# Attention and a cosine-gated MLP on one core: first output stage in visits of 2, 2, 2, 1, lower transfer figures in the planner, the last MLP pair in halves, and the inverse sums stored by SyncE

## The chip, the core and the metric

The kernel runs on one core of one Trainium2 chip. The metric is the device time of one execution in microseconds (us). Five engines work side by side and meet only at semaphores: TensorE (PE, matmuls), ScalarE (ACT, activations), VectorE (DVE), GpSimd (POOL) and SyncE (SP, which here only issues transfers). ACT and POOL can issue transfers too. Each engine runs its own list of instructions in order, so an instruction that waits holds everything behind it on that engine.

## What is computed

```python
q_n = q / (norm(q) + 1e-6); k_n = k / (norm(k) + 1e-6)      # (8, 12, 448, 64) each
attn = softmax(q_n @ k_n.T / tau)                           # tau = 0.1
x = (attn @ v) as (8 * 448, 12 * 64) = (3584, 768)
h = x @ w_in                                                # (768, 2048)
out = (h * cos(h)) @ w_out                                  # (2048, 768), float32
```

## The kernel before, in words

**Tiling.** A *quad* is two pairs of heads of one batch; there are 24 quads (NQ), three for each of the eight batches. A quad's 448 keys are seven *groups* of 64 (NJ = 7), numbered g = 7 * quad + j. For each group, `scores` (L551) makes four 64x64-tile matmuls into two PSUM banks and ACT takes the exponential of both banks into one of 17 tiles E (L567); `attend` (L570) multiplies E with V and accumulates the quad's seven groups in banks X and Y (4 and 5). When the quad is complete, DVE copies the result to AVs (L586). Scores go alternately to banks 0, 1 and 2, 3, so PE can be at most two groups ahead of ACT's exponentials.

**Sums.** The softmax's sums are made later, in *rounds* of one or two quads (ROUNDS, L733: quad 3 alone, then 4 and 5, 6 and 7, and so on): `sums` (L630) adds up the E tiles with matmuls against a selector (L642), ACT takes Ln and Exp(-x) of the 448 columns (L649, L651), which gives the inverse sums in Zs, a small transfer stores them in DRAM (rscr, L652), and broadcasting loads bring them back to all partitions as R (L658, two per quad, issued by SP). POOL (DVE for quad 5) then multiplies AVs with R, which gives the quad's part of xT (L662). Quads 0 to 2 go another way in the prologue (`spread`, `scale_x`), using the tiles ar.

**Norms.** For each quad SP loads Q and K (Qf, Kf, L398, 448 KB each), POOL squares (L450), DVE reduces (L454), ACT and DVE make the inverse norms (L480 to L493), POOL scales (L501), and SP turns the result with DMA transposes into qT and kT (`turn`, L539, L544). A quad's turn may begin when the scores of the quad two before it are done, since there are two qT and kT.

**MLP.** For each batch c, `m1_part` (L670) makes 16 blocks of h (128 hidden columns each, six matmuls a block, L676) in eight pairs of banks, and `m1` (L683) makes h * cos(h) of a pair of blocks with four instructions over both banks: ACT rounds h / 2 pi to an integer (L689), DVE subtracts (L691), ACT takes the sine (L693), DVE multiplies into gT (L695). `m2` (L698) multiplies gT with w_out, 16 matmuls for each output tile of 128 rows and half of the columns (L704); DVE copies the tile out (L722) and SP stores it (L728).

**Order.** PE's order is the program's. After the prologue (quads 0 to 2), stage c does the MLP's first product of batch c, then its *output stage*: *visits*, each made by `group` (L756), of up to two groups of scores with the attends of the visit before, and between the visits `fill` (L953) puts matmuls of `m2`, and the sums that are due. QUADS (L731) gives the quads begun in each stage: 5, 4, 3, 3, 3, 3, 0, 0. In the first stage (c = 0) the visits cover groups 21 to 55: one group, then 17 times two, so quads of seven groups are straddled by every second visit (L975). There 20 matmuls of `m2` come first, 8 after the first visit, and 4 after each of the others. After the first visit of that stage the squares of a spare quad are added and `norm_b` of quad 5 is put in the list (L981). A round becomes due when a visit starts a quad (L773).

The other engines' order is made by a list scheduler, `Planner` (L22): every operation has an estimated duration, a latency and a priority worked back from PE's order; a transfer's estimate is 1.2 us, its `moves` figure and 0.8 us (FIRST, LAST), its ring being one of SP, ACT and POOL (`land`, L70). SWITCH (L32) is the estimated cost of a change between matmul shapes on PE. The estimates do not reach the chip: they only set the order in which ACT, DVE, POOL and SP get their instructions, and where semaphores are waited for. `lead` (15 for the sums' operations) raises a priority.

Of the kernel before, what the change touches and what calls it, by code (L numbers as in the profile page):

```python
# [8 lines left out]
ACT = mybir.ActivationFunctionType  # L9
# [12 lines left out]
class Planner:  # L22
# [6 lines left out]
    ENGINES = ("pe", "act", "dve", "pool", "sp")  # L29
    HOP = {"pe": 0.055, "act": 0.045, "dve": 0.035, "pool": 0.08, "sp": 0.15}  # L30
    LAT = {"pe": 0.165, "act": 0.103, "dve": 0.085, "pool": 0.045, "sp": 0.0}
    SWITCH = 0.093  # L32
    FIRST, LAST = 1.2, 0.8
    WORTH = 1.0

# [236 lines left out]
def bass_cosine_attention__then__act_gcu_kernel(  # L272
# [110 lines left out]
    def cut(kind, u, part):  # L383

        return [(kind, u, i) for i, (j0, j1) in enumerate(CELLS) if part[0] < j1 and j0 < part[1]]
# [7 lines left out]
    def load_one(qd, w, part=ALL[0], after=(), eng="sp"):  # L393
        b, h0, s = qd // QB, 2 * (qd % QB), qd % 3
        src, dst, nm = ((q, Qf, "Qf"), (k, Kf, "Kf"))[w]
        j0, j1 = part
        ap = bass.AP(src.tensor, (b * NH + h0) * S * D + j0 * D, [[NJ * D, 128], [NH // 2 * S * D, 2], [1, (j1 - j0) * D]])
        return op(eng, 0.5, lambda e: e.dma_start(dst[s].ap()[:, :, j0:j1].rearrange("p r j d -> p r (j d)"), ap),  # L398
                  w=cut(nm, s, part), dma=(nm, s, j0), moves=0.196 * (j1 - j0), after=after, keep=qd > 4)

    def load_qk(qd, after=()):
        return [load_one(qd, w, after=after) for w in range(2)]
# [4 lines left out]
    def load_v(qd, after=()):  # L407
        b, h0, s = qd // QB, 2 * (qd % QB), qd % NV
        ap = bass.AP(v.tensor, (b * NH + h0) * S * D, [[NJ * D, 128], [NH // 2 * S * D, 2], [1, NJ * D]])
        return pool_dma(0.75, lambda e: e.dma_start(Vb[s].ap().rearrange("p r j d -> p r (j d)"), ap),  # L410
                  w=[("V", s)], dma=("V", s), moves=1.67, after=after)

    NW, WARM = 2, 34

    def load_w1(i, hf, after=()):
        w = FF // NW
        if 1:
            src = bass.AP(moe_w_in.tensor, hf * NKC * D * FF + i * w, [[FF, D], [D * FF, NKC], [1, w]])
            dst = W1.ap()[64 * hf:64 * hf + 64, :, i * w:i * w + w]
            return pool_dma(0.69, lambda e, src=src, dst=dst: e.dma_start(dst, src),  # L420
                     w=[("W1", i, hf)], dma=("W1", i, hf), moves=4.26, after=after)

    def load_w2(i, hf):
        src = moe_w_out.rearrange("(f p) n -> p f n", p=128)[:, 8 * i:8 * i + 8, HW * hf:HW * hf + HW]
        return pool_dma(0.79, lambda e: e.dma_start(W2.ap()[:, 8 * i:8 * i + 8, HW * hf:HW * hf + HW], src),
                 w=[("W2", i, hf)], dma=("W2", i, hf), moves=5.18)

    H, NLEAD, FAST = 2 * NJ, 5.0, 7
    SPARE = FIRST + 3
# [109 lines left out]
    def turn(qd):  # L539

        u = qd % 2
        turned[qd] = []
        for n, t, nm in ((Qn, qT, "Q"), (Kn, kT, "K")):
            turned[qd].append(op("sp", 1.3, lambda e, n=n, t=t: e.dma_start_transpose(  # L544
                t[u].ap().rearrange("p j a x -> p j (a x)"), n[u].ap().rearrange("p j r d -> p (j r d)")),
               r=cut(nm + "n", u, ALL[0]), w=cut(nm + "T", u, ALL[0]), dma=(nm + "T", u), moves=1.61, keep=True))

    summed = set()
    holds = {}
# [37 lines left out]

    Z, LEAD = 6, 15.0

    def spread(qd, j0, j1):  # L590

        s = qd % 3
        gs = range(NJ * qd + j0, NJ * qd + j1)

        def mm(e):
            for g in gs:
                for a in range(2):
                    for r in range(2):
                        ins = e.matmul(bank(Z + a, S, 64 * r, 64 * r + 64), ones.ap()[64 * a:64 * a + 64, :],
                                       E[g % NE].ap()[64 * a:64 * a + 64, r, :],  # L600
                                       start=(g == NJ * qd), stop=(g == NJ * qd + NJ - 1))
            return ins

        op("pe", 0.19 * (j1 - j0), mm, r=[("E", g % NE) for g in gs] + ["ones"], w=pair(Z), mode="q")
        if j1 < NJ:
            return
        summed.add(qd)
        act("exp", 0.815, lambda e: e.activation(ar[s].ap(), two(Z), ACT.Ln, bias=0.0, scale=1.0), r=pair(Z), w=[("ar", s)])
        act("exp", 0.83, lambda e: e.activation(ar[s].ap(), ar[s].ap(), ACT.Exp, bias=0.0, scale=-1.0),
            r=[("ar", s)], w=[("ar", s)])  # L610

    def scale_x(qd):
        b, c0, s = qd // QB, 2 * (qd % QB), qd % 3
        op("dve", 1.01, lambda e: e.tensor_tensor(xT[b % 2].ap()[:, c0:c0 + 2, :], two(X), ar[s].ap(), ALU.mult),
           r=pair(X) + [("ar", s)], w=[("x", b % 2, qd % QB)])

    def stir(qd, n):

# [11 lines left out]
    def sums(quads, bk):  # L630
        n = rounds[0]
        rounds[0] += 1
        summed.update(quads)
        z = n % 2
        np_ = 2 * len(quads)
        rows = 2 * np_

        def mm(e):
            for j in range(NJ):
                for i in range(np_):  # L640
                    es = (quads[i // 2] * NJ + j) % NE
                    ins = e.matmul(bank(bk, S, 32 * i, 32 * i + 32), sel.ap(), E[es].ap()[:, i % 2, :],  # L642
                                   start=(j == 0), stop=(j == NJ - 1))
            return ins

        op("pe", 1.32, mm, r=[("E", (qd * NJ + j) % NE) for qd in quads for j in range(NJ)] + ["sel"], w=whole(bk),
           mode="s")
        zz = Zs[z].ap()[0:32 * np_, :]
        act("exp", 0.44, lambda e: e.activation(zz, bank(bk, S, 0, 32 * np_), ACT.Ln, bias=0.0, scale=1.0),  # L649
            r=whole(bk), w=[("Zs", z)], lead=LEAD)  # L650
        act("exp", 0.47, lambda e: e.activation(zz, zz, ACT.Exp, bias=0.0, scale=-1.0), r=[("Zs", z)], w=[("Zs", z)], lead=LEAD)  # L651
        op("act", 0.6, lambda e: e.dma_start(rscr.ap()[8 * n:8 * n + rows, :], Zs[z].ap()[0:32 * np_:16, :]),  # L652
           r=[("Zs", z)], w=[("rs", n)], dma=("rs", z), moves=0.05, lead=LEAD)
        for i, qd in enumerate(quads):
            u, sl, b = qd % 2, qd % NA, qd // QB
            for r in range(2):
                ap = bass.AP(rscr, (8 * n + 4 * i + 2 * r) * S, [[0, 64], [S, 2], [1, S]])
                op("sp", 0.5, lambda e, r=r, u=u, ap=ap: e.dma_start(R[u].ap()[64 * r:64 * r + 64], ap),  # L658
                   r=[("rs", n)], w=[("R", u, r)], after=spared, dma=("R", u, r), moves=0.85, lead=LEAD)
            c0 = 2 * (qd % QB)  # L660
            late = qd == 2 * QB - 1
            op("dve" if late else "pool", 1.02 if late else 2.04, lambda e, u=u, sl=sl, b=b, c0=c0: e.tensor_tensor(  # L662
                xT[b % 2].ap()[:, c0:c0 + 2, :], AVs[sl].ap(), R[u].ap(), ALU.mult),
                r=[("AV", sl), ("R", u, 0), ("R", u, 1)], w=[("x", b % 2, qd % QB)], lead=LEAD)
# [18 lines left out]
    def m1(c, pr, bk):  # L683
        s = pairs[0] % 3
        pairs[0] += 1
        col = S * (c % 2)
        bs = pair(bk)

        op("act", 0.815, lambda e: e.activation(ar[s].ap().bitcast(I32), two(bk), ACT.Identity, bias=0.25, scale=INV2PI),  # L689
           r=bs, w=[("ar", s)])  # L690
        op("dve", 1.005, lambda e: e.scalar_tensor_tensor(ar[s].ap(), ar[s].ap().bitcast(I32), -2.0 * math.pi, two(bk),  # L691
                                                          ALU.mult, ALU.add), r=bs + [("ar", s)], w=[("ar", s)])
        act("sin", 0.86, lambda e: e.activation(ar[s].ap(), ar[s].ap(), ACT.Sin, bias=GUARD * math.pi / 2.0, scale=GUARD),  # L693
            r=[("ar", s)], w=[("ar", s)])
        op("dve", 1.01, lambda e: e.tensor_tensor(gT.ap()[:, 2 * pr:2 * pr + 2, col:col + S], two(bk), ar[s].ap(), ALU.mult),  # L695
           r=bs + [("ar", s)], w=[("g", c % 2, 2 * pr), ("g", c % 2, 2 * pr + 1)])

    def m2(t, h, f0, f1, bk):  # L698
        col = 128 * t % GC
# [10 lines left out]
        if f1 == NNB and t == B * S // 128 - 1:  # L710
# [3 lines left out]
            for sg, eng in enumerate(("sp", "act" if h else "sp")):  # L714
# [1 line left out]
                dst = bass.AP(out.tensor, (S * b + cc // 64) * KM + HW * h, [[NJ * KM, 64], [1, HW]])  # L716
                op(eng, 0.5, lambda e, sg=sg, dst=dst: e.dma_start(
                    dst, osb[so].ap()[64 * sg:64 * sg + 64, HW * h:HW * h + HW]),
                   r=[("o", so, h)], w=[("out", t, sg, h)], dma=("store", t, h, sg), moves=0.32)
        elif f1 == NNB:  # L720
            so = t % 3
            op("dve", 0.475, lambda e: e.tensor_copy(osb[so].ap()[:, HW * h:HW * h + HW], bank(bk, HW)),  # L722
# [1 line left out]
            if h:  # L724
                for sg in range(2):
                    b, cc = divmod(128 * t + 64 * sg, S)
                    dst = bass.AP(out.tensor, (S * b + cc // 64) * KM, [[NJ * KM, 64], [1, KM]])
                    op("sp", 0.5, lambda e, sg=sg, dst=dst: e.dma_start(dst, osb[so].ap()[64 * sg:64 * sg + 64, :]),  # L728
                       r=[("o", so, 0), ("o", so, 1)], w=[("out", t, sg)], dma=("store", so, sg), moves=0.66)

    QUADS = [5, 4, 3, 3, 3, 3, 0, 0]  # L731
    W, MOST = (1, 1), 9
# [186 lines left out]
    for c in range(B):  # L919
# [52 lines left out]
                m2(t, h, f0, f1, bank_of[t, h])  # L972

        new = done + QUADS[c]
        todo = [range(max(g, NJ * done), min(g + 2, NJ * new)) for g in range(NJ * done - (c == 0), NJ * new, 2)]  # L975
        more = new > done
        done = new
        if todo:
# [49 lines left out]
```

## Time and profile before

| | |
|---|---|
| three runs | 442.67, 439.15 and 441.56 us; median 441.56 |
| the profiled execution | 439.9 us, its span 438.3 us |
| granted TensorE clock, mean | 0.996 |
| PE, ACT, DVE, POOL busy | 419.0, 310.9, 255.7, 211.7 us of the span |
| prologue and c = 0's first product | 0 to 56.2 us |
| first output stage (c = 0) | 56.2 to 100.4 us |
| c = 1's first product begins | 101.31 us |
| c = 7's last output matmuls | to 434.5 us |

The table is of one profiled execution; its times are microseconds from the span's start. In the lines of the profile that follow, a line of a timeline has the start, the duration, the engine, the line of the code, the operation, the tile written and the tile read, and in brackets the idle time before it with what ended it. A `q` behind the name of an engine (SPq, ACTq) marks the issue of a transfer, which is not counted as busy time.

### The profile page before, as it was taken

The numbers are of one execution on the slowest core, as the hardware profiler recorded it, in microseconds if no ns is written. First come the engines' busy times: TensorE is split into PE (matmuls) and PEld (weight loads), VectorE is DVE, ScalarE is ACT, GpSimd is POOL, SyncE is SP. The second block draws the span as 40 slices with busy tenths as digits, with TensorE's granted clock in tenths as the row PEclk, the third lists the DMA queues.
The fourth block names the chain that finished last, engine by engine and source line by source line (L and its number), as shares of the span: only waits on it lengthen the run. The fifth ranks groups of instructions, "written<-read, shape, count | busy, mean of one in ns | idle before, by whom it ended". The sixth has DMA issues, their size and how long they took to land.

```text
span 438.3 us, 8435 instructions
## 1 busy us (share of the span) xinstructions
PE 419.0 (96%) x3578; PEld 208.3 (48%) x3578; DVE 255.7 (58%) x300; ACT 310.9 (71%) x432; POOL 211.7 (48%) x145
## 2 busy tenths in 40 slices
PE   7889998989999899999999999999999999999996
PEld 7344542334544345444454454444554445565563
DVE  4865993246972349923696329933585225935931
ACT  4898877897788777788679766878678757704700
POOL 3888545659347778277636773149633033000000
PEclk9999998999999999999999999999999999999999
DMA  7999995797918979276952995067931614021022
GB/s 255 238 255 222 272 193 112 172 224 168 203 55 187 235 167 247 45 167 152 237 159 61 236 237 139 0 137 188 221 71 38 159 42 122 1 73 37 0 72 73
DMA packets 70942, 64.34 MB, mean 147 GB/s; under 512 B 40100, under 2 KB 63224, under 8 KB 70904
## 3 DMA queue, kind: packets, MB, share of 16 engines
q1 hardware_dynamic: 57824, 51.30, 47.5%
q0 software_dynamic: 12288, 11.80, 17.9%
q10 hardware_dynamic: 792, 0.71, 0.5%
q8 instruction: 28, 0.46, 0.4%
q14 instruction: 10, 0.08, 0.1%
HBM read 55.25 MB, written 11.16 MB: 152 GB/s over the span
## 4 chain that ended last, share of the span: by engine, by line
PE 82%; ACT 7%; DVE 4%; issue 3%; DMA 1%; POOL 1%; SPq 1%; ACTq 1%; POOLq 0%
PE PS L676 33%; PE PS L704 31%; PE PS L560 7%; PE PS L577 6%; ACT E L567 4%; PE PS L642 3%; DMA Qf<-in_q_dram 1%; DVE n L454 1%; DVE gT L695 1%; SPq L544 1%; ACTq L652 1%; DVE osb L722 1%; ACT Zs L651 1%; ACT Zs L649 1%; POOL xT L662 0%
## 5 line engine op out<-in xcount | busy, mean ns | idle before, releaser
L704 PE MATMUL PS<-W,gT 128*128 128x384 bf16 x896 | 162.3, 328 | 0.1
L567 ACT ACTIVATE E<-PS 128x896 bf16<-128x896 f32 x168 | 144.6, 916 | 24.5 <-PE PS L560 20.1
L676 PE MATMUL PS<-xT,W 128*128 128x448 bf16 x768 | 147.7, 353 | 0.9 <-POOL xT L662 0.9
L704 PEld LDWEIGHTS PS<-W,gT 128*128 128x128 bf16 x896 | 81.0, 98 | 77.9 <-issue 26.2
L676 PEld LDWEIGHTS PS<-xT,W 128*128 128x128 bf16 x768 | 74.4, 98 | 72.0 <-issue 1.7
L689 ACT ACTIVATE ar<-PS 128x896 int32<-128x896 f32 x64 | 58.2, 911 | 46.0 <-PE PS L676 46.0
L691 DVE SCALAR_TENSOR_TENSOR ar<-ar,PS 128x896 f32<-128x896 int32 x64 | 69.2, 1082 | 28.7 <-ACT ar L689 28.6
L722 DVE COPY osb<-PS 128x384 f32<-128x384 f32 x54 | 30.0, 556 | 76.9 <-PE PS L704 75.9
L695 DVE TENSOR_TENSOR gT<-PS,ar 128x896 bf16<-128x896 f32 x64 | 69.5, 1087 | 1.5 <-ACT ar L693 1.0
L693 ACT ACTIVATE ar<-ar 128x896 f32<-128x896 f32 x64 | 60.6, 946 | 13.4 <-DVE ar L691 13.4
L560 PE MATMUL PS<-qT,kT 64*64 64x448 bf16 x672 | 61.8, 365 | 6.2 <-ACT E L567 3.4
L662 POOL TENSOR_TENSOR xT<-AVs,R 128x896 bf16<-128x896 f32 x20 | 41.6, 2091 | 45.3 <-DMA R<-rscr 45.2
L450 POOL TENSOR_TENSOR sqq<-Qf 128x896 bf16<-128x896 f32 x21 | 35.2, 1678 | 53.4 <-DVE n L454 37.6
L577 PE MATMUL PS<-E,Vb 64*64 64x448 bf16 x672 | 48.6, 355 | 3.4 <-ACT E L567 3.2
L450 POOL TENSOR_TENSOR sqk<-Kf 128x896 bf16<-128x896 f32 (+1 forms) x22 | 36.5, 1660 | 24.1 <-DVE n L454 15.4
L501 POOL TENSOR_TENSOR Qn<-Qf,rr 128x896 bf16<-128x896 f32 x21 | 36.3, 1728 | 19.8 <-ACT rr L493 19.6
L586 DVE COPY AVs<-PS 128x896 f32<-128x896 f32 x21 | 22.8, 1085 | 35.6 <-PE PS L577 35.6
L560 PEld LDWEIGHTS PS<-qT,kT 64*64 64x64 bf16 x672 | 18.8, 105 | 39.0 <-ACT E L567 15.0
L501 POOL TENSOR_TENSOR Kn<-Kf,rr 128x896 bf16<-128x896 f32 (+1 forms) x22 | 36.6, 1666 | 0.5 <-DVE Qn L501 0.5
L454 DVE TENSOR_REDUCE n<-sqq 128x14 f32<-128x896 bf16 (+2 forms) x24 | 24.9, 1039 | 6.4 <-POOL sqq L450 6.3
L454 DVE TENSOR_REDUCE n<-sqk 128x14 f32<-128x896 bf16 (+2 forms) x24 | 25.0, 1041 | 5.3 <-POOL sqk L450 5.2
L577 PEld LDWEIGHTS PS<-E,Vb 64*64 64x64 bf16 x672 | 19.2, 107 | 17.3 <-ACT E L567 9.0
(53 smaller groups left out, 175.6 us busy)
## 6 DMA issues: line engine op xcount, KB each, us to landing
Qf<-in_q_dram SPq DMA_DIRECT2D x24, 448.0 KB, 6.0
out_dram<-osb SPq DMA_DIRECT2D x54, 192.0 KB, 2.9
Kf<-in_k_dram SPq DMA_DIRECT2D x23, 448.0 KB, 6.7
R<-rscr SPq DMA_DIRECT2D x42, 224.0 KB, 4.5
Vb<-in_v_dram POOLq DMA_DIRECT2D x24, 224.0 KB, 5.8
W<-in_moe_w_in_dram POOLq DMA_DIRECT2D x4, 768.0 KB, 17.7
W<-in_moe_w_out_dram POOLq DMA_DIRECT2D x4, 768.0 KB, 31.9
Kf<-in_k_dram ACTq DMA_DIRECT2D x1, 320.0 KB, 6.1
```

Source lines behind the costliest of these rows:

```text
L450: op(eng, (1.68 if eng == "pool" else 1.05) * n, lambda e: e.tensor_tensor(dst, src, src, ALU.mult), r=cut(nm + "f", s, part), w=at, after ...
L454: return op("dve", 0.07 + 0.95 * n, lambda e: e.tensor_reduce(out=n2[u].ap()[:, H * w:H * w + H] if part == ALL[0] else jr(n2[u], w, part) ...
L501: lambda e: e.tensor_tensor(n[u].ap()[:, j0:j1].rearrange("p j r d -> p r j d"), f[s].ap()[:, :, j0:j1], rb, ALU.mult),
L560: ins = e.matmul(bank(bs + r, S, 64 * a, 64 * a + 64), kT[u].ap()[64 * r:64 * r + 64, j, a, :], qT[u].ap()[64 * r:64 * r + 64, :, a, :], s ...
L567: act("exp", 0.875, lambda e: e.activation(E[es].ap(), two(bs), ACT.Exp, bias=0.0, scale=INV_TAU), r=pair(bs), w=[("E", es)], chain="E")
L577: ins = e.matmul(bank((X, Y)[a], S, 64 * r, 64 * r + 64), Vb[vs].ap()[64 * a:64 * a + 64, r, j, :], E[es].ap()[64 * a:64 * a + 64, r, :], ...
L676: ins = e.matmul(bank(bk + i2), W1.ap()[:, i, 128 * nb:128 * nb + 128], xT[c % 2].ap()[:, i, :], start=(i == 0), stop=(i == NKC - 1))
L689: op("act", 0.815, lambda e: e.activation(ar[s].ap().bitcast(I32), two(bk), ACT.Identity, bias=0.25, scale=INV2PI), r=bs, w=[("ar", s)])
L691: op("dve", 1.005, lambda e: e.scalar_tensor_tensor(ar[s].ap(), ar[s].ap().bitcast(I32), -2.0 * math.pi, two(bk), ALU.mult, ALU.add), r=bs ...
L693: act("sin", 0.86, lambda e: e.activation(ar[s].ap(), ar[s].ap(), ACT.Sin, bias=GUARD * math.pi / 2.0, scale=GUARD), r=[("ar", s)], w=[("a ...
L695: op("dve", 1.01, lambda e: e.tensor_tensor(gT.ap()[:, 2 * pr:2 * pr + 2, col:col + S], two(bk), ar[s].ap(), ALU.mult), r=bs + [("ar", s)] ...
L704: ins = e.matmul(bank(bk, HW), gT.ap()[:, f, col:col + 128], W2.ap()[:, f, HW * h:HW * h + HW], start=(f == 0), stop=(f == NNB - 1))
```

## The change

Four things are changed.

1. In the first output stage each quad gets its own visits, of 2, 2, 2 and 1 groups: 20 visits in place of 18, and none straddles two quads.
2. The planner's figures: `moves` is about a fifth lower for all transfers, and SWITCH goes from 0.093 to 0.115.
3. In `m1`, the last of the eight pairs (blocks 14 and 15) is worked in two halves of one bank each: eight instructions over 448 columns in place of four over 896. The tiles ar are tracked by halves for that, also where the prologue uses them.
4. The small transfer that stores a round's inverse sums in DRAM is issued by SP in place of ACT, so it uses SP's ring.

```diff
-    SWITCH = 0.093
+    SWITCH = 0.115
...
-                  w=cut(nm, s, part), dma=(nm, s, j0), moves=0.196 * (j1 - j0), after=after, keep=qd > 4)
+                  w=cut(nm, s, part), dma=(nm, s, j0), moves=0.157 * (j1 - j0), after=after, keep=qd > 4)
...
-               r=cut(nm + "n", u, ALL[0]), w=cut(nm + "T", u, ALL[0]), dma=(nm + "T", u), moves=1.61, keep=True))
+               r=cut(nm + "n", u, ALL[0]), w=cut(nm + "T", u, ALL[0]), dma=(nm + "T", u), moves=1.29, keep=True))
...
+    def ars(s, i0=0, i1=2):
+        return [("ar", s, i) for i in range(i0, i1)]
...
-        op("act", 0.6, lambda e: e.dma_start(rscr.ap()[8 * n:8 * n + rows, :], Zs[z].ap()[0:32 * np_:16, :]),
+        op("sp", 0.5, lambda e: e.dma_start(rscr.ap()[8 * n:8 * n + rows, :], Zs[z].ap()[0:32 * np_:16, :]),
...
-                   r=[("rs", n)], w=[("R", u, r)], after=spared, dma=("R", u, r), moves=0.85, lead=LEAD)
+                   r=[("rs", n)], w=[("R", u, r)], after=spared, dma=("R", u, r), moves=0.68, lead=LEAD)
...
-        op("act", 0.815, lambda e: e.activation(ar[s].ap().bitcast(I32), two(bk), ACT.Identity, bias=0.25, scale=INV2PI),
-           r=bs, w=[("ar", s)])
...
+        def some(i0, i1):
+            n = i1 - i0
+            bs = [x for i in range(i0, i1) for x in whole(bk + i)]
+            src = two(bk)[:, i0:i1]
+            a, ai = ar[s].ap()[:, i0:i1], ar[s].ap().bitcast(I32)[:, i0:i1]
+            at = ars(s, i0, i1)
+            op("act", 0.195 + 0.31 * n, lambda e: e.activation(ai, src, ACT.Identity, bias=0.25, scale=INV2PI), r=bs, w=at)
...
+        for part in ((0, 1), (1, 2)) if pr == NNB // 2 - 1 and True else ((0, 2),):
+            some(*part)
...
-        todo = [range(max(g, NJ * done), min(g + 2, NJ * new)) for g in range(NJ * done - (c == 0), NJ * new, 2)]
+        todo = [range(g, min(g + 2, NJ * new)) for g in range(NJ * done, NJ * new, 2)]
+        if c == 0:
+            todo = [range(NJ * qd + i, NJ * qd + min(i + 2, NJ)) for qd in range(done, new) for i in range(0, NJ, 2)]
```

The lines left out lower the other `moves` figures (V from 1.67 to 1.34, w_in 4.26 to 3.41, w_out 5.18 to 4.14, output stores 0.66 to 0.53 and 0.32 to 0.26), use `ars` in `spread` and `scale_x`, and write the other three instructions of `some` (subtract, sine, multiply) in the same manner.

## The prediction, made before the changed kernel was run

> **What bounds the kernel now.** I read the page first: shares of busy time, then the chain that ended last.
>
> ```profile
> PE 419.0 (96%) x3578; PEld 208.3 (48%) x3578; DVE 255.7 (58%) x300; ACT 310.9 (71%) x432; POOL 211.7 (48%) x145
> ...
> PE 82%; ACT 7%; DVE 4%; issue 3%; DMA 1%; POOL 1%; SPq 1%; ACTq 1%; POOLq 0%
> ```
>
> TensorE is busy 96% and makes 82% of the chain, so a change that leaves the matmuls alone can only win the holes. Next the windows by stage (columns: length, then PE, PEld, DVE, ACT, POOL busy, granted clock, DMA share, GB/s): most of the first output stage (visits and sums of c = 0), and that of c = 3 to compare.
>
> ```profile
> 62.70:97.00 34.30, 29.21 (x327) 10.65 (x326) 14.10 (x20) 28.84 (x43) 20.63 (x15) 0.95 0.87 168
> ...
> 227.00:259.60 32.60, 32.60 (x322) 16.01 (x320) 15.87 (x19) 26.61 (x40) 20.19 (x13) 1.00 0.66 163
> ```
>
> The first stage has 5.1 us of PE idle and a clock of 0.95; c = 3 has none. The same table gives idle 1.25 in c = 1, 0.82 in c = 2, 0.81 in c = 4, and 0 in the output stages of c = 5, 6 and 0.02 in that of c = 7. So the change is decided in the first stage, with crumbs in three more. ACT's timeline there:
>
> ```profile
> 69.92 0.54 ACT L649 ACTIVATE Zs<-PS 64x448 f32<-64x448 f32 x1 [0.78 <-PE PS L642]
> 70.49 0.58 ACT L651 ACTIVATE Zs<-Zs 64x448 f32<-64x448 f32 x1
> 71.10 1.08 ACTq L652 DMA_DIRECT2D rscr<-Zs  x1
> 72.23 2.53 ACT L567 ACTIVATE E<-PS 128x896 bf16<-128x896 f32 x3 [1.16 <-issue]
> ```
>
> The exponential at 72.23 had its scores long before; 1.08 us of its delay is the issue of one transfer. PE's timeline and 2 us windows show what that costs:
>
> ```profile
> 73.20 0.38 PE L577 MATMUL PS<-E,Vb 64*64 64x448 bf16 x4 [2.06 <-ACT E L567]
> ...
> 74.55 0.59 PE L560 MATMUL PS<-qT,kT 64*64 64x448 bf16 x4
> ```
> ```profile
> 72.00:74.00 2.00, 0.80 (x10) 0.35 (x11) 0.01 (x1) 1.77 (x3) 0.70 (x1) 1.00 0.31 51
> 74.00:76.00 2.00, 2.00 (x20) 0.65 (x17) 0.56 (x1) 1.57 (x2) 0.00 (x0) 0.57 0.61 197
> ...
> 90.00:94.00 4.00, 2.61 (x33) 0.85 (x32) 2.20 (x3) 3.86 (x6) 1.08 (x1) 1.00 1.25 167
> ```
>
> PE stands 2.06 us, then runs at 0.57 from 74 to 78: four score matmuls show 0.59 us instead of 0.38. PE busy 65% of 90:94 drew no such drop. Last, the way into the next stage, on SP, POOL and PE:
>
> ```profile
> 86.90 2.05 SPq L544 DMA_TRANSPOSE kT<-Kn  x1
> 89.00 0.59 SPq L398 DMA_DIRECT2D Qf<-in_q_dram  x1
> 89.63 0.69 SPq L398 DMA_DIRECT2D Kf<-in_k_dram  x1
> 94.34 2.40 SPq L658 DMA_DIRECT2D R<-rscr  x4
> ```
> ```profile
> 95.89 1.68 POOL L450 TENSOR_TENSOR sqq<-Qf 128x896 bf16<-128x896 f32 x1 [4.82 <-DMA Qf<-in_q_dram]
> ...
> 99.17 2.08 POOL L662 TENSOR_TENSOR xT<-AVs,R 128x896 bf16<-128x896 f32 x1
> ```
> ```profile
> 101.31 4.71 PE L676 MATMUL PS<-xT,W 128*128 128x448 bf16 x24 [0.92 <-POOL xT L662]
> ```
>
> PE is ready for c = 1's first product at 100.39 and waits 0.92 us for POOL's xT. That xT follows the chain sums (86.12), ACT (to 88.83), store to rscr (issued 88.86, landed about 94.3, when SP goes on), R loads, POOL.
>
> **The change part by part.**
>
> *Store of the inverse sums on SP (L652).* It takes eleven issues of 0.55 to 1.08 us from ACT. Four are on the chain: 1.08 at 71.10, 0.55 at 146.78, 0.47 at 187.54, 0.57 at 287.62. In c = 2 the loss can be read directly:
>
> ```profile
> 187.44 0.57 ACTq L652 DMA_DIRECT2D rscr<-Zs  x1
> ...
> 188.06 3.35 ACT L567 ACTIVATE E<-PS 128x896 bf16<-128x896 f32 x4 [0.53 <-ACT rr L493]
> ```
> ```profile
> 189.03 0.38 PE L560 MATMUL PS<-qT,kT 64*64 64x448 bf16 x4 [0.43 <-ACT E L567]
> ...
> 189.84 0.38 PE L577 MATMUL PS<-E,Vb 64*64 64x448 bf16 x4 [0.24 <-ACT E L567]
> ```
>
> PE waits 0.43 + 0.24 behind an issue of 0.57: gain 0.55. The same two waits (0.43, 0.23) stand in c = 4: 0.55. In c = 1 only 0.23 follows the issue: 0.23. At the other seven issues ACT had slack (it waits about 0.7 us per visit for PE in c = 3 and 5) or the gain falls into the chain below. Sum outside the first stage: -1.33. Late next there is nothing until the next osb copy: in c = 1 PE waits 0.88 for it, unchanged.
>
> In the first stage the PE hole of 2.06 shrinks by 1.08 to about 1.0. PE busy in 70:74 was 1.14 + 0.80 = 1.94 of 4 us; it becomes about 3.0, above the 2.61 that kept the clock. I therefore take the drop as gone: 4 us at 0.57 lose PE 1.7 us, of which ACT, the other bound there, felt its waits for PE (0.43, 0.20, 0.83), 1.46. So groups after 31 come 1.08 + 1.46 = 2.5 us earlier; bounds 1.08 (drop stays) and 2.8 (all of the 1.7). The Trainium skill, "TensorE: Matmul & The Clock Gate", Part 1, says that the gate judges activity in free-running windows of about 3.4 us and otherwise halves the clock; the trace agrees in length (0.57 over 74 to 78) and by that rule the drop goes too, unless the window falls badly.
>
> Price on SP: one issue, 0.5 to 0.6 us, ahead of the R loads, and a wait for ACT's exponential. Behind it stand the R loads, which wait for the store anyway, and later turns, loads and output stores. In the trace SP waits 26.1 us before R loads and 166.9 us for output tiles, so the issue itself costs nothing; without that cover it costs 0.6 per round. What can cost is its place in SP's ring. For round [4,5] the Q and K loads of quad 9 become free to issue right after the turn of quad 7, that is before the sums. On ACT's ring the store landed at 94.3, after kT (86.90 + 7.2 = 94.1) but before Qf (89.0 + 6.4 = 95.4) and Kf (89.63 + 7.2 = 96.8). Behind both on SP's ring it lands at about 96.9, +2.6. R for quad 4 then lands near 100.9 (two issues of 0.6, 3.4 to land), POOL's xT ends at 103.0 instead of 101.25: +1.75. If it is ahead of the loads it lands with kT as now: +0, or -0.92 if xT then no longer holds PE. I take +1.3, nearer the row where the loads stand in front, and keep -0.92 and +1.75. Round [8,9] of c = 1 has the same picture, milder: landed 152.0, Kf 152.4, and its xT is 2.3 us early (158.5 against 160.8).
>
> *Visits 2, 2, 2, 1 in the first stage.* 20 visits instead of 18. A change of matmul shape costs 0.10 us each way: four L704 start at 82.65 and the next scores at 83.40, 0.75 where 4 x 0.163 = 0.65. Two visits more are four changes, +0.4. Before sums [4,5] there are 12 visits in place of 11, so 4 more output matmuls come earlier (+0.65) and as many fewer after. The single visit carries one exponential (0.84) against PE's 0.2 + 0.38 + 0.65 + 0.2 = 1.4, so ACT runs dry up to 0.6 us per quad, five times; against it the first visit starts two exponentials at once, where ACT waited 1.25 at 62.25 for a reduction: one exponential (0.84) won. The attend groups that straddle two quads (12 matmuls after an AVs copy, 0.22 wait) go. Up to group 28 I find gain and loss equal, after it the transposes hide what a single loses (kT of quad 7 held PE 0.87 at 94.15; one more visit gives it time). Taken +0.2 for the part of the 0.4 ahead of the sums; bounds -1.5 (the 0.84 and 0.87 both won) and +2.5 (0.6 dry in four quads).
>
> *Last pair in halves.* Per stage two more ACT and two more DVE instructions: 0.54 twice against 0.92 (the 448 column Ln is 0.54), 0.56 twice against 1.08, together about +0.4 ACT, +0.1 DVE, hidden: ACT next waits for PE or DVE. No PE matmul waits for gT anywhere in the list of waits (PE reaches block 14 at 124.9, gT is done at 124.4), so nothing is won there; ACT's table load comes some 0.4 earlier, where exponentials wait 0.05 to 0.1 for it. Taken -0.1, bounds +0.4 and -0.4.
>
> *Planner figures.* No work is added. Loads are now put at 3.1 instead of 3.4 us, transposes 3.3 instead of 3.6; the trace has 3.7 to 7.5 and 2.9 to 7.3. The figures move away from the trace, so ready work may stand behind late data more often, as POOL's 4.82 us on Qf. Only in the first stage is that near the path; PE's own order is fixed. Taken 0, bounds -1 and +1.9 (POOL's 4.82 less what R's landing hides).
>
> **Sum.** First stage: -2.5 + 0.2 + 1.3 = -1.0; this is also about what xT allows: 103.05 - 2.3 = 100.7 against 101.31, so of PE's 2.5 the rest is given back at the join. Elsewhere -1.33, halves -0.1: -2.5. I round up for the straddling groups and the 0.87 wait, partly won: -2.8. The profiled execution took 439.9 (span 438.3 and 1.6 around it), so 437.1; the median of the runs is 1.66 above it, so 441.56 - 2.8 = **438.8**.
>
> **Rivals.** 1. *The whole first stage heals*: the store gets ahead of the loads, PE's 5.1 us idle falls to about 1.5 and the clock stays: -3.6 - 1.5 + 0.4, with -1.4 elsewhere, -6.1: 435.5. For it: c = 2 runs at 0.82 idle with the same helpers. Against: ACT has 28.84 of 34.30 us of work there, and the loads are ready first. 2. *Slower: the store behind the loads holds c = 1.* If xT ends at 103.0 without moving earlier (the turn and loads being late as now), +1.75; PE, there by 98, stands 5 us, its clock drops as at 74, +1.7; with +0.4 for switches and -1.4 elsewhere, +2.5: 444.0. It decides once the store lands over 3 us later after the sums than now. For it: Kf landed 2.5 us after the store. Against: turn and loads hang on scores that come earlier. The Trainium skill, "DMA: Bandwidth & Descriptors", Queues, rings and completion order, says that descriptors of one ring are consumed in order and rings take turns, which speaks against moving the store; the trace shows the store overtaking Qf and Kf from its own ring. 3. *Nothing moves*: the new order brings as many new stalls as the 2.67 us of issues on the chain were worth: 441.5. For it: a list scheduler's order shifts everywhere at once, and the figures get less true.
>
> **Chances.** Forecast 0.5, rival 1 0.23, rival 2 0.15, rival 3 0.12. The forecast alone spans 437 to 440.5. Leaving out the outer part of rivals 1 and 2, the range is 435.2 to 443.6. One per cent is 4.4 us, about what a measurement here can tell from no change. Faster by it (under 437.1): rival 1 and a little of the forecast, 0.29. Slower by it (over 446.0): the worse part of rival 2, where the lost clock is joined by the singles' bound of +2.5, 0.11. Within: 0.60.
>
> **What would show it.** Right: no store on ACT's queue, ACT's Ln, Exp and exponential in a row after the first sums; PE's wait there near 1.0; clock 1.00 through 70 to 78; the pairs of waits in c = 2 and 4 gone; the join into c = 1 within 1 us of the path. Wrong: a clock drop elsewhere in the first stage, R issued more than 8.2 us after sums [4,5] began, PE waiting over 2 us for xT, ACT dry after each single visit, or new PE waits in stages that had none.

## The result, and the profile after

Twelve runs of each kernel: 439.81 us (median, 436.23 to 442.40) after, 441.67 us (439.15 to 446.34) before. The ratio is 0.9947, with a 95% interval of 0.9922 to 0.9973: 2.3 us faster, between 1.2 and 3.4 (the medians alone differ by 1.9). The forecast was 2.8 us. All ratios leave out executions more than 1.5% above the fastest of the same kernel; of the kernel with the figures alone, below, these are four of twelve, its profiled one among them.

The two profiled executions do not show this gain in their spans (438.3 and 438.6 us). That of before was 1.8 us under its median, that of after 0.6 us over. So the profiles are read stage by stage, and the ratios for the sums. The page of the changed kernel:

```profile
PE 420.0 (96%) x3578; PEld 208.9 (48%) x3578; DVE 256.1 (58%) x316; ACT 311.5 (71%) x448; POOL 211.4 (48%) x145
...
PE 80%; ACT 6%; DVE 4%; DMA 4%; issue 2%; POOL 2%; SPq 0%; POOLq 0%
```

ACTq is gone from the chain and SPq is 0% of it; DMA has grown from 1% to 4%. The windows, with the same columns as before:

```profile
62.70:97.00 34.30, 32.19 (x362) 11.54 (x360) 16.23 (x23) 31.32 (x48) 24.03 (x18) 1.00 0.98 199
...
72.00:74.00 2.00, 2.00 (x28) 0.60 (x20) 0.48 (x1) 1.98 (x3) 0.67 (x1) 1.00 0.15 23
74.00:76.00 2.00, 2.00 (x30) 0.83 (x23) 0.44 (x2) 1.84 (x4) 0.01 (x1) 1.00 0.72 224
...
96.00:98.00 2.00, 0.00 (x0) 0.00 (x0) 0.21 (x1) 1.72 (x7) 1.40 (x1) 1.00 0.95 144
98.00:100.00 2.00, 1.28 (x5) 0.61 (x6) 1.96 (x2) 1.34 (x2) 2.00 (x2) 0.81 0.18 28
100.00:102.00 2.00, 2.00 (x7) 0.83 (x6) 0.08 (x1) 0.00 (x0) 2.00 (x2) 0.50 0.34 75
```

The hole and the clock drop of 70 to 78 are gone. In their place PE stands still at 96 to 98, and the clock drops after that. ACT's timeline at the first sums:

```profile
67.73 1.73 ACT L567 ACTIVATE E<-PS 128x896 bf16<-128x896 f32 x2
69.53 0.54 ACT L652 ACTIVATE Zs<-PS 64x448 f32<-64x448 f32 x1
70.10 0.58 ACT L654 ACTIVATE Zs<-Zs 64x448 f32<-64x448 f32 x1
70.61 4.39 ACT L567 ACTIVATE E<-PS 128x896 bf16<-128x896 f32 x5
```

No issue follows the Exp, and the list now has two exponentials ahead of the Ln where there was one, so PE has no hole at all here. The new visits do the second: with the old ones and the store on SP (`u_visits`, `sp_figs` and `a_sp` below) the hole is 0.78 us. Now the join into c = 1, on SP, POOL and PE (the first product is L679 here, xT L665, the store L655, R L661):

```profile
85.37 0.58 SPq L398 DMA_DIRECT2D Qf<-in_q_dram  x1
86.00 0.49 SPq L398 DMA_DIRECT2D Kf<-in_k_dram  x1
86.53 0.62 SPq L655 DMA_DIRECT2D rscr<-Zs  x1
...
91.28 2.39 SPq L661 DMA_DIRECT2D R<-rscr  x4
```
```profile
96.60 2.06 POOL L665 TENSOR_TENSOR xT<-AVs,R 128x896 bf16<-128x896 f32 x1 [0.79 <-DMA R<-rscr]
```
```profile
98.72 6.40 PE L679 MATMUL PS<-xT,W 128*128 128x448 bf16 x24 [2.78 <-POOL xT L665]
```

The store stands behind Qf and Kf of quad 9. R is issued 8.7 us after the sums began (82.54), where it was 8.2. PE is ready at 95.94 in place of 100.39, waits 2.78 us, and then takes 6.40 us for 24 matmuls that took 4.71.

What POOL does just ahead of xT matters as much as the store. In the kernel before, POOL came to xT (99.17) straight from the squares of quad 9, which had waited 4.82 us for Qf; the second R load of quad 4, issued at 94.94, had landed about 0.2 us earlier. Now R is the later of the two, by the 0.79 us shown. Had R been early, POOL would still have been at those squares and the issue of a load of V until 95.81, and PE would have waited about 2.0 us (an estimate from these rows).

Times between the starts of the first products, in the two profiles, with the forecast's part of each:

| stretch | before | after | difference | forecast |
|---|---|---|---|---|
| start to c = 0 | 37.04 | 37.09 | 0.05 | 0 |
| c = 0 to c = 1 | 64.27 | 61.63 | -2.64 | -1.0 |
| c = 1 to c = 2 | 58.00 | 59.06 | 1.06 | -0.23 |
| c = 2 to c = 3 | 48.96 | 48.31 | -0.65 | -0.55 |
| c = 3 to c = 4 | 51.23 | 53.00 | 1.77 | 0 |
| c = 4 to c = 5 | 48.95 | 50.01 | 1.06 | -0.55 |
| c = 5 to the end | 129.85 | 129.50 | -0.35 | 0 |

The 1.7 us of the clock drop at the join stand in the row c = 1 to c = 2. The halves (-0.1) and the 0.3 that the forecast added by rounding stand in no row.

### The profile page after: what moved, and what is told of

Read it like the earlier page. It is cut to its first block, busy times and chain, and to the rows that moved or that the text cites. A ratio compares the mean times of both kernels' runs of the same rounds, so it can differ in the third digit from the quotient of the medians.

```text
span 438.6 us, 8468 instructions
## 1 busy us (share of the span) xinstructions
PE 420.0 (96%) x3578; PEld 208.9 (48%) x3578; DVE 256.1 (58%) x316; ACT 311.5 (71%) x448; POOL 211.4 (48%) x145
## 4 chain that ended last, share of the span: by engine, by line
PE 80%; ACT 6%; DVE 4%; DMA 4%; issue 2%; POOL 2%; SPq 0%; POOLq 0%
PE PS L679 33%; PE PS L715 29%; PE PS L560 7%; PE PS L577 6%; ACT E L567 4%; PE PS L645 3%; DMA Qf<-in_q_dram 2%; DVE n L454 1%; DMA rscr<-Zs 1%; DMA R<-rscr 1%; DVE gT L703 1%; DVE osb L733 1%; DVE ar L698 0%; POOL xT L665 0%; PE PS L602 0%
## 5 line engine op out<-in xcount | busy, mean ns | idle before, releaser
L679 PE MATMUL PS<-xT,W 128*128 128x448 bf16 x768 | 149.4, 355 | 2.8 <-POOL xT L665 2.8
L679 PEld LDWEIGHTS PS<-xT,W 128*128 128x128 bf16 x768 | 74.8, 98 | 74.9 <-issue 3.5
L697 ACT ACTIVATE ar<-PS 128x896 int32<-128x896 f32 (+1 forms) x72 | 58.7, 827 | 48.7 <-PE PS L679 48.7
L698 DVE SCALAR_TENSOR_TENSOR ar<-ar,PS 128x896 f32<-128x896 int32 (+1 forms) x72 | 69.2, 978 | 28.2 <-ACT ar L697 28.1
L703 DVE TENSOR_TENSOR gT<-PS,ar 128x896 bf16<-128x896 f32 (+1 forms) x72 | 69.5, 983 | 1.4 <-ACT ar L700 1.0
L700 ACT ACTIVATE ar<-ar 128x896 f32<-128x896 f32 (+1 forms) x72 | 60.7, 862 | 12.5 <-DVE ar L698 11.8
L665 POOL TENSOR_TENSOR xT<-AVs,R 128x896 bf16<-128x896 f32 x20 | 41.5, 2084 | 43.5 <-DMA R<-rscr 43.4
L454 DVE TENSOR_REDUCE n<-sqq 128x14 f32<-128x896 bf16 (+2 forms) x24 | 24.9, 1038 | 10.9 <-POOL sqq L450 10.8
```

The source lines that it names most:

```text
L454: return op("dve", 0.07 + 0.95 * n, lambda e: e.tensor_reduce(out=n2[u].ap()[:, H * w:H * w + H] if part == ALL[0] else jr(n2[u], w, part) ...
L679: ins = e.matmul(bank(bk + i2), W1.ap()[:, i, 128 * nb:128 * nb + 128], xT[c % 2].ap()[:, i, :], start=(i == 0), stop=(i == NKC - 1))
L697: op("act", 0.195 + 0.31 * n, lambda e: e.activation(ai, src, ACT.Identity, bias=0.25, scale=INV2PI), r=bs, w=at)
L698: op("dve", 0.06 + 0.47 * n, lambda e: e.scalar_tensor_tensor(a, ai, -2.0 * math.pi, src, ALU.mult, ALU.add), r=bs + at, w=at)
L700: act("sin", 0.22 + 0.32 * n, lambda e: e.activation(a, a, ACT.Sin, bias=GUARD * math.pi / 2.0, scale=GUARD), r=at, w=at)
L703: op("dve", 0.07 + 0.47 * n, lambda e: e.tensor_tensor(gT.ap()[:, f0:f1, col:col + S], src, a, ALU.mult), r=bs + at, w=[("g", c % 2, f) fo ...
```

## The experiments

Ratios are to the kernel before, of runs on the same chip; the changed kernel is 0.9947. "Undo" kernels take one part out of the changed kernel.

**Undo the store on SP (u_act).**

```diff
-        op("sp", 0.5, lambda e: e.dma_start(rscr...
+        op("act", 0.6, lambda e: e.dma_start(rscr...
```

> The changed kernel with the store of the inverse sums back on ACT. The theory of the forecast (the issues on ACT held exponentials on the chain, in the first stage with a clock drop behind one) expects most of the gain lost: 0.998 to 1.003 of the kernel before, a PE hole of over 1 us after the first sums, and the pairs of PE waits (0.43 and 0.24 us) back in c = 2 and c = 4. The rival (the store's place in SP's ring is what the join into c = 1 waits for, 2.78 us and a clock drop, and the visits alone heal the first stage) expects a faster kernel than the changed one: 0.988 to 0.992, with PE's wait for xT under 1 us and no clock drop at 99 us.

Measured 0.9995 (0.9968 to 1.0023): the gain is gone, as the theory had it. The pairs of waits of c = 2 and c = 4 are back (0.41 and 0.24 in both), but the hole after the first sums is only 0.42 us, since the two exponentials still go ahead of the Ln. The first stage has another hole:

```profile
96.59 0.57 PE L577 MATMUL PS<-E,Vb 64*64 64x448 bf16 x8 [2.13 <-DVE AVs L586]
102.09 4.70 PE L679 MATMUL PS<-xT,W 128*128 128x448 bf16 x24
```

R is issued at 91.56, 6.6 us after its sums (85.01), and PE does not wait for xT. So the rival was right about the join, and wrong that this decides: a hole of 2.13 us with a clock drop behind it took the place. In the two profiles the way from c = 0's first product to c = 2's is then as long with the store on ACT (120.75 us) as on SP (120.69). Of the 2.1 us between the two ratios the profiles place only 0.64, in c = 2; where the rest is lost stays open.

**Undo the visits (u_visits)**: the old expression for `todo`.

> The changed kernel with the first stage's visits as before (one group, then two each, straddling quads). The forecast's theory (visits cost 0.4 us of switches and win about as much) expects no change against the changed kernel: 0.993 to 0.996 of the kernel before, and PE at the join at about 96 us as in the changed kernel (95.9). The rival (the visits by quad are what closed the holes of the first stage) expects 0.997 to 1.001, and PE at the join at 98 us or later.

Measured 0.9948 (0.9914 to 0.9983), the changed kernel's own figure. PE is ready at the join 59.0 us after c = 0's first product began, against 58.9 (at 98.1 on the clock of the profile, since that product began 2.0 us later in this execution). The visits close the hole at the first sums, as said above, and still are worth nothing that can be measured here.

**Undo the figures (u_figs)**: the nine old values of `moves` and SWITCH.

> The changed kernel with the planner's old figures (moves and SWITCH). The forecast's theory (figures only reorder, worth nothing on the sum) expects 0.992 to 0.997 of the kernel before. The rival (the lower figures put work behind late transfers: the new PE waits of 1.69 us at 251 for a copy behind a reduction that waits for Qf, and of 1.75 us at 300 for a turn) expects both waits gone and 0.985 to 0.990.

Measured 1.0122 (1.0084 to 1.0159), against both theories. SP's list of the first stage and what PE met:

```profile
84.71 3.82 SPq L544 DMA_TRANSPOSE kT<-Kn  x1
88.57 0.58 SPq L398 DMA_DIRECT2D Qf<-in_q_dram  x1
89.20 0.73 SPq L398 DMA_DIRECT2D Kf<-in_k_dram  x1
89.97 1.27 SPq L655 DMA_DIRECT2D rscr<-Zs  x1
...
94.11 1.26 SPq L544 DMA_TRANSPOSE qT<-Qn  x1
98.41 2.39 SPq L661 DMA_DIRECT2D R<-rscr  x4
```
```profile
95.66 0.59 PE L560 MATMUL PS<-qT,kT 64*64 64x448 bf16 x4 [4.60 <-DMA kT<-Kn]
108.02 4.29 PE L679 MATMUL PS<-xT,W 128*128 128x448 bf16 x11 [4.57 <-POOL xT L665]
```

Here qT and kT of quad 7 landed 11.8 and 10.9 us after their issue, R was issued 14.3 us after the sums (84.08), and PE waited over 4.5 us twice, at half clock after each. The list for PE is the same in both kernels, to the instruction; those of the other engines are not. SP issues R between the halves of quad 8's turn (94.11 and 102.02), and at the first sums in the same way between those of quad 6's. POOL takes scalings of quads 8 and 9 ahead of xT, so xT began only at 105.06, about 2 us after the R loads of quad 4 had landed. How much each of these costs was not tried apart. Of the two later waits, which the rival expected gone, that at 251 is gone, while one of 1.60 us ahead of a quad's scores in c = 4 remains.

**Undo the halves (u_pair)**: the last pair in one piece.

> The changed kernel with the last MLP pair in one piece again. The forecast's theory (hidden work, no PE wait for gT) expects no change against the changed kernel: 0.993 to 0.996 of the kernel before. The rival (the halves let ACT and DVE reach the first visit's work earlier in each of six stages) expects 0.997 to 1.000.

Measured 0.9973 (0.9951 to 0.9995), between the two. The interval overlaps with the changed kernel's; whether the halves win up to about 1 us is not settled.

**The store on SP alone, on the kernel before (a_sp).**

> The kernel before with only the store of the inverse sums moved to SP. The theory of the forecast (the issue leaves ACT and the store costs about 1 us at the join) expects 0.993 to 0.999 of the kernel before. The rival, formed on the run with the old figures (with them, SP's list puts halves of the turns and the store behind loads, and PE waits over 4 us for kT and for xT), expects 1.005 to 1.015, and a PE wait of over 3 us at the join into c = 1.

Measured 1.0051 (1.0018 to 1.0084): slower, as the rival said. PE's timeline:

```profile
71.91 0.38 PE L577 MATMUL PS<-E,Vb 64*64 64x448 bf16 x4 [0.78 <-ACT E L567]
...
100.06 7.18 PE L676 MATMUL PS<-xT,W 128*128 128x448 bf16 x24 [3.88 <-POOL xT L662]
```

The hole at the first sums shrinks from 2.06 to 0.78 and no drop follows: the forecast's mechanism by itself. PE is ready at 96.18, 4.2 us sooner. But xT ends at 100.0, PE stands 3.88 us, and the clock drop costs 2.5 (7.18 against 4.71). The store buys time in the first stage and the join gives all of it back. The store's landing is not the whole cause, as POOL shows:

```profile
96.29 1.68 POOL L501 TENSOR_TENSOR Qn<-Qf,rr 128x896 bf16<-128x896 f32 x1 [2.03 <-ACT rr L493]
97.94 2.06 POOL L662 TENSOR_TENSOR xT<-AVs,R 128x896 bf16<-128x896 f32 x1
```

The scaling of quad 8 now stands ahead of xT in POOL's list, and it waits for inverse norms from ACT. The R loads of quad 4 had landed by 96.6, so about 1.3 us of the 3.88 are this order's (an estimate from these rows). In the kernel before and in the changed one POOL takes xT first.

**The figures alone, on the kernel before (a_figs).**

> The kernel before with only the planner's figures lowered (moves and SWITCH). The theory of the forecast (no work added, order only) expects 0.998 to 1.002 of the kernel before. The first rival (the figures are worth by themselves what taking them back cost, 1.75%) expects 0.983 to 0.990; the second (they matter only for a store that is on SP, whose ring they describe) agrees with the forecast's number, but with SP's list in the first stage nearly unchanged.

Measured 1.0049 (1.0013 to 1.0085): slower than any of the three expected, though the interval's lower end reaches into the first's. The order of the instructions in its profile shows the lists. SP's in the first stage is nearly the old one, as the second rival said: one pair of output stores stands later, behind the loads of quad 9. POOL's and DVE's lists change in more places. Why the figures alone lose stays open.

**Store and figures together, on the kernel before (sp_figs).**

> The kernel before with two of the four parts: the store on SP and the lower figures. The theory now (the gain is these two together: the store off ACT, and a list for SP that keeps each turn whole and frees the R loads early; visits and halves are worth nothing) expects 0.993 to 0.997 of the kernel before, although each of them alone gave 1.005. The rival (visits or halves are needed as well) expects 0.999 to 1.005.

Measured 0.9957 (0.9922 to 0.9991). Each alone loses 0.5%, both together win 0.4%, which is most or all of the change. The parts do not add. As the theory says, SP's list here keeps each turn whole and has R ahead of quad 8's turn; POOL's has xT ahead of quad 8's scaling again.

**Undo SWITCH only (u_switch)**, 0.115 back to 0.093.

> The changed kernel with SWITCH alone back at 0.093, the transfer figures staying lower. If the transfer figures (moves) make SP's list, as the theory has it, 0.993 to 0.997 of the kernel before, as the changed kernel; if SWITCH does, 1.005 to 1.015, as with all old figures, and PE waits of over 4 us for kT and xT in the first stage.

Measured 0.9945 (0.9910 to 0.9979): with the other parts in place it is the transfer figures that matter, and SWITCH does not. PE waits 2.17 us for xT in its profile, and there the clock stays: the 24 matmuls take 4.71.

**The wait at the join filled with matmuls (j_warm).**

```diff
+        if c == 1:
+            hold(38, at_bank[0])
```

`hold`, left out here, issues the given number of 128x128x128 matmuls of the identity into the bank that the first product then overwrites.

> The changed kernel with 38 small matmuls of the identity on PE ahead of c = 1's first product, into a bank that is free; the result is untouched. They take about 2.3 us, inside the 2.78 us in which PE waits for xT. The theory (that wait drops the clock to a half for 3.4 us, which costs 1.7 us) expects the first 24 matmuls of c = 1 in 4.6 us instead of 6.4, no drop there, and 0.989 to 0.992 of the kernel before. The rival (c = 1 gives the time back, since ACT or the transfers hold its visits) expects 0.993 to 0.997.

Measured 0.9886 (0.9850 to 0.9922), 435.87 us. PE's timeline and its windows:

```profile
96.15 2.29 PE L801 MATMUL PS<-ident 128*128 128x128 bf16 x38
98.27 4.70 PE L679 MATMUL PS<-xT,W 128*128 128x448 bf16 x24
```
```profile
98.00:100.00 2.00, 2.00 (x18) 1.18 (x16) 1.43 (x2) 0.29 (x1) 2.00 (x2) 1.00 0.01 1
```

The first product starts 0.45 us earlier than in the changed kernel, and its first 24 matmuls take 4.70 us in place of 6.40: the drop costs 1.7 us, as priced. The rest of the 2.7 us between the ratios is within their intervals; in the profiles, c = 3 and c = 4 are 2.9 us shorter together.

This kernel also shows what the new PE waits of c = 3 and c = 4 were. Its lists for SP, DVE and ACT are the changed kernel's; POOL's differs in one place, a scaling of Q at 77.37 that the changed kernel has at 80.75, behind the xT of quad 3. In the changed kernel POOL, DVE and PE show, one after the other:

```profile
247.39 1.68 POOL L450 TENSOR_TENSOR sqq<-Qf 128x896 bf16<-128x896 f32 x1 [3.14 <-DMA Qf<-in_q_dram]
```
```profile
249.10 1.09 DVE L454 TENSOR_REDUCE n<-sqq 128x14 f32<-128x896 bf16 x1 [2.70 <-POOL sqq L450]
250.10 1.08 DVE L586 COPY AVs<-PS 128x896 f32<-128x896 f32 x1
```
```profile
251.24 0.57 PE L577 MATMUL PS<-E,Vb 64*64 64x448 bf16 x8 [1.69 <-DVE AVs L586]
```

The AVs copy stands behind a reduction that waits, through POOL, for Qf. In the kernel before, DVE has the copy first:

```profile
249.82 1.09 DVE L586 COPY AVs<-PS 128x896 f32<-128x896 f32 x1 [1.12 <-PE PS L577]
250.83 1.07 DVE L454 TENSOR_REDUCE n<-sqq 128x14 f32<-128x896 bf16 x1
```

In the changed kernel Qf landed 8.1 us after its issue at 239.20; with the filled wait it took 5.8, POOL waited 0.97, and PE not at all (c = 3 took 51.11 us, not 53.00). In the same way a kT that landed 6.5 us after its issue (3.9 before) cost PE 1.75 at 300. How long these waits are depends on the landing times, but they are not the accident of one execution. With the lower figures and the halves together the copy stands behind the reduction, and PE waits for it in c = 3 in the profiles of the changed kernel and of `u_act`, `u_visits`, `u_switch`, `j_ahead` and `j_ahead2` (1.27 to 1.69 us; c = 3 took 52.6 to 53.0 us). Without one of the two, in the kernel before, `a_sp`, `u_figs`, `u_pair` and `sp_figs`, c = 3 took 51.1 to 51.2. The two filled kernels have the reduction first as well, with a wait of 0.22 us or none.

**The store ahead of the loads (j_ahead).** The loads of quad 9 are created behind the store, which SP must issue in that order.

```diff
-                if FIRST < qd < NQ - 4:
+                if FIRST < qd < NQ - 4 and qd != 5:
...
+                   ... lead=LEAD, keep=quads[0] == 4)
+        if quads[0] == 4:
+            load_qk(9)
```

> The changed kernel with the store of round [4,5] put ahead of the loads of quad 9 in SP's list. The theory (the store lands behind the 896 KB that stand before it in SP's ring) expects it to land with the turn of quad 7, SP to go on with R 2 us or more sooner after the sums (8.67 us in the changed kernel), PE to wait under 1 us for xT, no clock drop, and 0.985 to 0.990 of the kernel before. The rival (SP stands waiting for the store's semaphore, and the R loads or the loads of quad 9 come late in its place) expects 0.994 to 1.000, with a longer wait for xT, or a new one for the turns of c = 1.

In this form the squares of quad 9 stand ahead of its loads and use what the tiles held before, so the result is not the kernel's and POOL does not wait for the loads. Measured 0.9924 (0.9889 to 0.9959); in its profile PE did not wait for xT and the clock stayed at 1.00. As the squares wait for nothing here, this says little of the order of the store. It does show R without loads in front of it: the two R loads of quad 4 landed 3.3 and 3.8 us after their issue, against 4.4 and 4.7 in the changed kernel.

**The same with the squares behind the loads (j_ahead2).**

> The store of round [4,5] ahead of the loads of quad 9 in SP's list, this time with the squares of quad 9 put behind those loads. As for the first form: the theory (the store lands behind what stands before it in SP's ring) expects SP to issue R under 6.7 us after the sums began, PE to wait under 1 us for xT, the first 24 matmuls of c = 1 in 4.7 us, and 0.985 to 0.990 of the kernel before; the rival (the loads of quad 9 come late in its place, or SP stands waiting) expects 0.994 to 1.000.

Measured 0.9981 (0.9949 to 1.0013): the rival's figure, with its mechanism half right. SP and POOL:

```profile
85.29 0.61 SPq L655 DMA_DIRECT2D rscr<-Zs  x1
85.95 0.44 SPq L398 DMA_DIRECT2D Qf<-in_q_dram  x1
86.43 1.85 SPq L398 DMA_DIRECT2D Kf<-in_k_dram  x1
88.50 2.43 SPq L664 DMA_DIRECT2D R<-rscr  x4
```
```profile
96.03 2.06 POOL L668 TENSOR_TENSOR xT<-AVs,R 128x896 bf16<-128x896 f32 x1 [2.37 <-DMA R<-rscr]
```

The store does land sooner: R is issued 6.1 us after the sums (82.40), not 8.7. But R itself now travels behind Qf and Kf: quad 4's landed 6.5 and 6.9 us after issue, and xT starts at 96.03 against 96.60. So the 896 KB of loads are the delay, ahead of the store or behind it. PE waits 2.35 us and the clock drops.

**A second filled wait (warm_switch)**: 34 small matmuls and SWITCH at 0.093.

> The changed kernel with SWITCH at 0.093 (0.9945 of the kernel before without more) and 34 small matmuls of the identity ahead of c = 1's first product, a second trial of the filled wait with other lists on ACT and POOL. The theory (the filled wait keeps the clock, which dropped in most executions) expects 0.988 to 0.992 of the kernel before and no drop at the join. The rival (the gain of the first trial was the luck of its transfers, or its own list on POOL) expects 0.993 to 0.997.

Measured 0.9859 (0.9811 to 0.9906), 435.04 us, no wait and no drop at the join. Both filled kernels beat the changed one: the best of its twelve executions was 436.23 us, and four of six of each filled kernel were below that, on chips where the kernel before had about the same median. The mean clock was 0.998 or more in all twelve filled executions; in nine of the changed kernel's twelve it was 0.996 or less. One rival is left: POOL's list has the same scaling moved forward in both filled kernels, so only the 1.7 us seen in the 24 matmuls is shown to be the filled wait's.

## Why the prediction was right in its number, and where its steps failed

*The store off ACT, outside the first stage: right.* Forecast -0.55 in c = 2, measured -0.65, both waits gone, and back with the store on ACT. In c = 4 the pair is gone too; the stage is longer only by the late kT.

*The hole and the drop at the first sums: right in kind, too small.* The hole was to be 1.0; by the store alone it is 0.78, with the new visits as well it is 0. The drop at 74 went in both. PE reaches the join 4.45 us sooner, not 2.3 (2.5 less the 0.2 for the visits). The windows of 62.70 to 97.00 show where: PE was idle 5.1 us before and 2.1 after, of which 1.06 is already the wait at the join. What the sum left out are the other 1.0 us of the hole and the waits of 0.43 and 0.23 behind the second issue, which I counted as lost in the chain, and of 0.87 for kT, which I rounded to "partly". All of them are gone.

*The join: the step that failed inside the first stage, and luck in the sum.* I took +1.3 for the store's place in SP's ring, as it was to land behind Qf and Kf, 2.6 us later. It did not: issued behind both, it had landed 4.8 us after its issue, ahead of Kf, and R went out only 0.5 us later after the sums than before. The trace of before, which I read as the store overtaking these loads, could not show that: it was issued at 88.86, ahead of Qf at 89.00. And the chain that I gave for xT left out POOL's squares of quad 9, which the lines show directly ahead of it. PE's wait grew all the same by 1.86 (2.78 less 0.92): xT ended 1.0 us later after the sums, behind the loads and the squares, and PE needed 0.9 us less from the sums to the join. The drop behind the wait, 1.7, I had put into rival 2 alone, as if only a join that makes the kernel slower could trip the clock. The sum is -4.45 + 1.86 + 1.70 = -0.9, where I had -1.0: errors of 2.1 and 2.3 us that cancel, by luck. Rival 2 was thus right about the wait and the drop and wrong in the balance; with the store alone its balance is what happens (+0.5%).

*The planner's figures: the other step that failed.* "Only in the first stage is that near the path; PE's own order is fixed. Taken 0, bounds -1 and +1.9." With the store on SP the old figures cost 7.7 us more than the new ones (1.0122 against 0.9947). I reasoned that figures further from the trace must be worse or nothing. Nearness to the trace did not decide: the lower figures happen to keep each turn whole in SP's list, R ahead of the next turn, and xT ahead of the next scaling in POOL's. They also reach beyond the first stage, by the copy behind the reduction in c = 3. The rest of the error is in the form of the sum: I priced the parts one by one and added. Store and figures alone are each +0.5%, together -0.4%.

*Visits: right* (taken +0.2; measured 0 within the intervals). *Halves: open*, -0.1 taken, 0 to about -1 measured.

*Rival 3* had its part: new waits of 1.69 in c = 3, which had none, and of 1.75 in c = 4, and the first recurs with the new lists.

*The signs, and the total.* Of the signs named for being wrong, three came: R issued 8.7 us after the sums, PE waiting 2.78 us for xT, and a new wait in a stage that had none. The forecast's own parts add to -2.43 before it rounds. In the profiled pair the stretches add to +0.3; the forecast's number agrees with the gain over many executions, in which the waits and the drop vary, and not with the pair that I took apart.

## What to carry to other kernels

Once list order decides, parts of a change do not add: a part that frees an engine and a part that reorders the queue it is moved to have to be priced, and tried, together. Time won inside a stage is worth what the join at its end lets through, so follow the longest chain of transfers to the join first, look at what stands just ahead of its last instruction on that engine, and count a clock drop with every PE wait of 2 us or more (nine of ten here). Where such a wait can't be shortened, harmless matmuls in it keep the clock: 1.7 us for a few lines here.

## What the runs showed of the hardware

- *The clock after short waits.* Behind the prologue, PE waits of 1.94 (`sp_figs`), 2.06 (before), 2.13 (`u_act`), 2.14 (`u_visits`), 2.35 (`j_ahead2`), 2.78 (after), 3.09 (`u_pair`), 3.88 (`a_sp`) and, in `u_figs`, 4.57 and 4.60 us were each followed by a drop to half clock. Waits of 1.92 (`sp_figs`) and 2.17 (`u_switch`) were not, nor any of those from 0.9 to 1.75 us. At the join, where 24 matmuls take 4.70 us, the drop cost 1.3 to 1.7 us after waits up to 3.09 and 2.5 to 2.7 after the longer ones. In the changed kernel's twelve runs, the three with a mean clock of 1.000 average 437.6 us, the nine others (0.991 to 0.996) 440.1. So part of the spread from run to run goes with clock drops. The join is not their only place: in the profiles of `u_act`, `u_visits` and `u_figs` the clock also fell in the prologue, to 0.66 to 0.77 over 16 to 20 us, and c = 0's first product began 1.5 to 2.1 us later than in the changed kernel's. The Trainium skill, "TensorE: Matmul & The Clock Gate", Part 1, has the gate judge free-running windows of about 3.4 us; the trace agrees in that the same wait may or may not drop the clock, and shows that waits well short of a window can do it.
- *Order in one ring.* The store, issued on SP behind Kf, had landed by 91.28, when SP went on, while Kf (86.00) landed 6.5 us after its issue, at 92.5. The Trainium skill, "DMA: Bandwidth & Descriptors", Queues, rings and completion order, says that completion is not FIFO per issuing engine; the trace agrees.
- *Landing times.* A turn's transpose of the same size took from 2.9 to 11.8 us to land in these traces, from 64 us of the span on. In the kernel before, it was 2.9 to 10.3 us there, and 3.6 to 9.3 for a load of Q or K: wider than the 2.9 to 7.3 and 3.7 to 7.5 that the prediction read.
